# Value products of eight heads in one stretch, and a narrower price for products that run beside others, in a planned transformer block

## The chip, the cores and the metric

The kernel runs on one core of one Trainium2 chip. The core has TensorE (PE, matrix products; PEld are its weight loads), VectorE (DVE), ScalarE (ACT), GpSimd (POOL), and queues that issue DMAs, of which SyncE (SP) issues most here. The metric is the device time of one execution in microseconds, median of several runs. Before the change it is 1022.17 us (3 runs, 1020.41 to 1023.81).

## What is computed

One transformer block with 2048 tokens of width 640: layernorm, attention of 32 heads of width 20 over a sliding window of 256 tokens, a residual, a second layernorm and a gated feed-forward of width 1536.

```python
h  = x + A(layernorm(x))          # A: qkv = x @ wqkv; 32 heads, Dh = 20, W = 256
#   scores = q k^T * Dh**-0.5; masked to 0 <= i - j < 256; p = softmax(scores)
#   out = (p v) @ wo
h2 = h + B(layernorm(h))          # B: (gelu(x @ w_gate) * (x @ w_up)) @ w_down
```

## The kernel before

**Tiles.** Tokens are cut into 16 blocks of 128 (a chunk is two blocks). Dense products run in 16-bit pieces: each operand is split into a high and a low float16 part, and three products (high-high, high-low, low-high) stand for one. Of a block j, the window holds the key blocks j-2, j-1 and j.

**Attention, per block and pair of heads.** Four steps follow each other.

1. `maxima` writes q k^T of a pair of heads into one of two double banks of PSUM (`ra`, `rb`). Head dimensions are on 60 rows, so products run in quarters of the array: 2 row halves (the two heads) by 2 column halves. `max_out` then takes the row maximum on VectorE, one fused operation a head: add the mask (`band`, or `mask` for the first two blocks), reduce by max into a column of `mx`, and write the sum itself to a scratch tile `junk`, of which there is a single buffer. The profile shows it as CUSTOM_DVE_ANT_0, followed by a short read of the accumulator.
2. When a block has all 32 maxima, they are turned by a PE transpose (`max_transpose`) and put as two more rows under the queries, so that the next product comes out with the maximum subtracted. Maxima run some 20 pairs ahead of scores (`LEAD`).
3. `scores` computes k q^T of a pair into `ra` or `rb` (62 rows, 12 products for a full window). `score_out` takes the exponential on ScalarE into the probability tile `pt`. When all four heads of a unit `u` are there, GpSimd zeroes what the mask forbids, with three `affine_select` for a full window and one for the first two blocks. Then the unit is put into the queue `valq`. `pt` has 3 buffers of four heads.
4. `value_lane` multiplies a unit's probabilities with the values: for each key block four products side by side, one for each head, on 32 columns of the array each. A full window has 3 such groups; in float32 each product shows as two instructions, so a unit is x24 in the timeline (x16 and x8 for the first blocks). Results lie in the PSUM bank `pv`, four units in it; after each fourth unit ScalarE copies it to `oT`, and the unit after that waits for the copy.

In the timeline, products with shape 60*64 are maxima, 62*64 scores, 128*21 values, and 128*128 dense products or transposes. Maxima and scores together are called row products here, values column products, and a run of one kind a stretch.

**What sets the order.** The program is written out by a planner in the kernel itself. `Clock` keeps a time for each engine and a price for each instruction (`Engine.cost`, lines 214 to 250). Work sits in generators ("lanes"), each of which says what its next instruction needs; the loop at the end asks the lanes in an order of priority, and issues the first that can start by the planned clocks. The prices therefore only set the order of the instructions. For TensorE the price has three parts: `SWITCH` = 0.095 us where the kind of stretch changes, the columns at 2400 per us, and a fixed small price for a product that runs beside the one before it on another part of the array (`beside`). On VectorE the planner lets an operation that touches what the operation before it wrote start 0.1 us later (line 111).

Dense products (`dense_lane`) and attention are weighed by `ahead`: as long as the dense lane is ahead of the scores, attention comes first. Value products have two rules of their own. While the array is in row mode they come before nearly everything, and with fewer than two units waiting they are kept from starting out of dense products:

```python
if nc.mode == "row":
    early = [values] + early
elif len(valq) < 2 and (maxq or scoreq):
    att_lanes = [rows]
```

`row_need` starts row products by twos where both double banks come free within 1 us of each other; it lets scores start only while a probability buffer is free.

Before the scores begin, the loop also issues products with the identity (`pv<-ident` in the profile) whenever TensorE has nothing to do.

After attention, the first feed-forward group fills gaps (`first_feed_forward`), and then the rest of the feed-forward runs.

All instructions are recorded at line 199, where the helper issues them.

## Time and profile before

| | |
|---|---|
| median of 3 runs | 1022.17 us (1020.41 to 1023.81) |
| the profiled execution | 1023.17 us, of which its span is 1021.3 us |
| granted TensorE clock | 1.00 throughout |
| instructions | 30777 |
| probability masking (`affine_select` on `pt`) | 352 instructions, 175.3 us of GpSimd |
| maxima (CUSTOM_DVE_ANT_0) | 512 operations; 448 of them on 320 columns |
| value products | 2880 instructions, 104.1 us busy, from 92.2 to 574.1 us |
| DMA | 112.67 MB, mean 110 GB/s |

Busy times are shares of the span. A PE matmul's duration is longer than its pitch, since products are pipelined: a product of 320 columns lasts 0.30 us in the rows, and the next one starts 0.136 us after it. So the start times, not the durations, are added up for TensorE. A timeline row gives the start in us, the duration, the engine, the line, the operation with output and inputs, its shape and how many instructions were merged; a square bracket gives idle time before it and what ended that.

The stages can be told by the spans of the tiles: weights and the first layernorms up to about 50 us, maxima of the first blocks from 52 us, value products from 92 to 575 us, and feed-forward alone from there to the end.

### The profile page before, as it was taken

The page shows a single profiled execution, that of the slowest core. Times are in us where ns is not written, and L with a number is a line of the kernel's source. Part 1 is how long each engine was busy: PE and PEld are TensorE (multiplying, and loading weights), DVE is VectorE, ACT ScalarE, POOL GpSimd, SP SyncE. Part 2 cuts the span into 40 slices and gives each one's busy share as a digit, 9 for nine tenths or more (in the row PEclk, how much of TensorE's full clock was granted, in tenths as well). Part 3 has the DMA queues.
Part 4 walks back from the last instruction along what each step waited for, and adds up shares of the span by engine and source line. Part 5 has one row for each costly group of instructions (what it writes and reads, how often), then busy time and mean ns, then how long its engine had stood idle before and what let it go on. Part 6 is the DMA issues. An engine that isn't in the chain of part 4 may idle for free.

```text
span 1021.3 us, 30777 instructions
## 1 busy us (share of the span) xinstructions
PE 999.8 (98%) x12921; PEld 695.8 (68%) x12921; DVE 754.8 (74%) x2221; ACT 437.0 (43%) x706; POOL 298.0 (29%) x489
## 2 busy tenths in 40 slices
PE   8999999999999999999999999999999999999998
PEld 7875666676666676776655564567777777777776
DVE  6888998986787787474788788798996975544553
ACT  6514654656555564654558543522222222221220
POOL 7102223443343342342436321255313310000000
PEclk9999999999999999999999999999999999999999
DMA  8657667361551524225033433223553532222211
GB/s 306 137 116 175 184 145 168 81 163 55 91 122 44 114 57 118 42 61 127 3 131 106 92 117 103 78 104 127 161 177 90 161 138 78 78 96 86 78 53 52
DMA packets 105835, 112.67 MB, mean 110 GB/s; under 512 B 38369, under 2 KB 79585, under 8 KB 105697
## 3 DMA queue, kind: packets, MB, share of 16 engines
q1 hardware_dynamic: 93600, 99.97, 35.9%
q10 hardware_dynamic: 12096, 10.75, 3.4%
q8 instruction: 101, 1.65, 0.7%
q14 instruction: 38, 0.30, 0.1%
HBM read 73.73 MB, written 28.84 MB: 100 GB/s over the span
## 4 chain that ended last, share of the span: by engine, by line
PE 82%; DVE 8%; DMA 4%; ACT 2%; issue 2%; SPq 1%; POOL 0%; ACTq 0%; DVEq 0%
PE mm L199 41%; PE pv L199 12%; PE ra L199 11%; PE rb L199 10%; PE tp L199 7%; DVE junk L199 2%; DVE am L199 1%; DVE ht L199 1%; DMA v<-in_wqkv_dram 1%; DMA gu<-in_wqkv_dram 1%; SPq L199 1%; DMA qT<-mT 1%; DVE m L199 1%; ACT pt L199 1%; DMA h_dram<-ht 1%
## 5 line engine op out<-in xcount | busy, mean ns | idle before, releaser
L199 POOL TENSOR_SCALAR_AFFINE_SELECT pt<-pt 128x512 f32<-128x512 f32 x352 | 175.3, 513 | 278.2 <-ACT pt L199 262.6
L199 DVE CUSTOM_DVE_ANT_0 junk<-rb,band 128x320 bf16<-128x320 f32 x230 | 112.5, 489 | 41.3 <-PE rb L199 35.9
L199 DVE CUSTOM_DVE_ANT_0 junk<-ra,band 128x320 bf16<-128x320 f32 x218 | 106.6, 489 | 43.8 <-PE ra L199 38.3
L199 ACT ACTIVATE pt<-ra,esc 128x640 f32<-128x640 f32 (+2 forms) x131 | 99.6, 767 | 66.2 <-PE ra L199 53.3
L199 ACT ACTIVATE pt<-rb,esc 128x640 f32<-128x640 f32 (+2 forms) x125 | 94.9, 766 | 77.2 <-PE rb L199 56.5
L199 PE MATMUL pv<-pt,v 128*21 128x128 f32 x2880 | 104.1, 275 | 1.1 <-ACT oT L199 1.1
L199 PEld LDWEIGHTS <-ah 128*128 128x128 f16 x768 | 75.0, 98 | 29.5 <-issue 2.1
L199 ACT ACTIVATE gel<-gel,ffk 128x512 f32<-128x512 f32 x36 | 26.0, 721 | 138.0 <-DVE gel L199 138.0
L199 PEld LDWEIGHTS pv<-pt,v 128*21 128x21 f32 x2880 | 68.6, 100 | 11.9 <-issue 2.1
L199 PEld LDWEIGHTS <-ws 128*128 128x128 f16 x720 | 70.3, 98 | 8.3
L199 PEld LDWEIGHTS <-kT 62*64 62x64 f16 x2880 | 61.9, 107 | 13.9 <-issue 10.1
L199 PEld LDWEIGHTS <-qT 60*64 60x64 f16 x1280 | 29.8, 104 | 60.3 <-issue 51.3
L199 PEld LDWEIGHTS <-gu 128*128 128x128 f16 x440 | 42.1, 98 | 36.1 <-issue 2.5
L199 DVE SCALAR_TENSOR_TENSOR ht<-mm,ffk,ht 128x320 f32<-128x320 f32 x96 | 52.1, 545 | 10.9 <-PE mm L199 9.0
L199 ACT CAST ah<-gel 128x512 f16<-128x512 f32 x48 | 29.6, 617 | 64.4 <-DVE gel L199 64.2
L199 PE MATMUL mm<-xh,w1h 128*128 128x256 f16 x200 | 54.7, 274 | 1.3 <-DVE qks L199 1.3
L199 PE MATMUL mm<-xl,w1h 128*128 128x256 f16 x200 | 54.7, 273 | 0.0
L199 PE MATMUL mm<-xh,w1l 128*128 128x256 f16 x200 | 54.7, 273 | 0.0
L199 PE MATMUL mm<-w3l,oh 128*128 128x320 f16 x160 | 48.1, 301 | 0.1
L199 PE MATMUL mm<-w2h,xh 128*128 128x320 f16 x160 | 48.1, 300 | 0.0
L199 PE MATMUL mm<-w2h,xl 128*128 128x320 f16 x160 | 48.1, 301 | 0.0
L199 PE MATMUL mm<-w3h,ol 128*128 128x320 f16 x160 | 48.1, 300 | 0.0
(299 smaller groups left out, 2521.3 us busy)
## 6 DMA issues: line engine op xcount, KB each, us to landing
ws<-wsums SPq DMA_DIRECT2D x24, 640.0 KB
qk<-qks ACTq DMA_DIRECT2D x32, 256.0 KB
qT<-qk SPq DMA_DIRECT2D x48, 160.0 KB
kT<-qk SPq DMA_DIRECT2D x48, 160.0 KB
wsums<-ws SPq DMA_DIRECT2D x12, 640.0 KB
ht<-in_x_dram SPq DMA_DIRECT2D x16, 320.0 KB
h_dram<-ht SPq DMA_DIRECT2D x16, 320.0 KB
ht<-h_dram SPq DMA_DIRECT2D x16, 320.0 KB
```

Source lines behind the costliest of these rows:

```text
L199: r = real(*args, **kw)
```

## The change

Four things are changed, and the sizes that follow from them.

- **Values by eight heads.** `value_lane` waits for two units in `valq` and issues both, one after the other, in one step, with one check of `pv` for both.
- **Probabilities in halves.** `pt` becomes 7 buffers of two heads. Masking on GpSimd is done for each half as soon as its exponential is there, with the same number of instructions for two heads as before for four. Scores may start while a half is free.
- **No scratch tile.** The maximum operation writes its sum back to where it read it, in PSUM, in float32; `mask` and `band` are bfloat16; an unused tile `ones` goes.
- **The order's price** of a product beside another is 0.0005 us and not 0.004 us.

```diff
             if beside:
-                return 0.004
+                return 0.0005
...
-    ones = const.tile([P, P], F32, name="ones")
-    nc.vector.memset(ones, 1.0)
...
-    mask = wp.tile([P, 2 * P], F32, name="mask")
+    mask = wp.tile([P, 2 * P], BF16, name="mask")
...
-    band = wp.tile([P, 5 * HB], F32, name="band")
+    band = wp.tile([P, 5 * HB], BF16, name="band")
...
-    RV, RK = 5, 6
+    RV, RK, RP = 5, 6, 7
...
-        free = 3 - (pos["units"] - pos["values"])
+        free = RP - (pos["parts"] - 2 * pos["values"])
         for j, pr in list(scoreq)[:2]:
             b = B[j]
-            free -= pr % 2 == 0
+            free -= pairs(j)
...
-            junk = at("junk", [P, 5 * HB], BF16, 1)
-            nc.vector.tensor_tensor_reduce(junk[:, :w], head,
+            nc.vector.tensor_tensor_reduce(head, head,
                                            band if n == 3 else mask[:, (2 - n) * P:], 1.0,
...
-        u = pr // 2
-        if pr % 2 == 0:
-            b.pt[u] = at("pt", [P, 4, 3, P], F32, 3)
-            pos["units"] += 1
+        for k in range(pairs(j)):
+            b.pt[pr + k] = at("pt", [P, 2, 3, P], F32, RP)
+        pos["parts"] += pairs(j)
...
+        for k in range(pr, pr + pairs(j)):
+            pt = b.pt[k]
+            yield on("gpsimd", pt[:, :, 0, :])
+            if n == 3:
+                half = pt.rearrange("p h a (b c) -> p h (a b) c", b=2)
+                for a, (i, o) in enumerate(((0, 0), (3, 5))):
+                    nc.gpsimd.affine_select(half[:, :, o], half[:, :, i],
+                                            pattern=[[0, 2], [-1, HB]], compare_op=ALU.is_ge,
+                                            fill=0.0, base=-1 - HB * a, channel_multiplier=1)
+            diag = part(pt, n, n - 1).rearrange("p h a b -> p h (a b)")
+            nc.gpsimd.affine_select(diag, diag, pattern=[[0, 2], [1, P]],
+                                    compare_op=ALU.is_ge, fill=0.0, base=0, channel_multiplier=-1)
+            pos[j, "u", k // 2] += 1
+            if pos[j, "u", k // 2] == 2:
+                valq.append((j, k // 2))
...
-            yield pe(when=lambda: valq and B[valq[0][0]].v == 2 and pos["ones"])
-            j, u = valq.popleft()
+            yield pe(when=lambda: len(valq) > 1 and B[valq[0][0]].v == 2 and pos["ones"])
+            j, u = valq[1]
...
-            yield pe(pt, pv[:, u % 4, :])
-            for k, i in enumerate(order):
-                for c in range(4):
+            yield pe(*(b.pt[k] for k in range(2 * u - 2, 2 * u + 2)),
+                     pv[:, u % 4 - 1:u % 4 + 1, :])
+            for u in (u - 1, u):
+                valq.popleft()
+                pt = [b.pt.pop(k) for k in (2 * u, 2 * u + 1)]
+                for k, i in enumerate(order):
+                    for c in range(4):
...
-            pos["values"] += 1
+                pos["values"] += 1
```

The two rules of the loop for value products are left as they are.

More of the change, by code (lines that the diff above doesn't have):

```diff
@@ L977, in scores @@
         t = t[:, :, :pairs(j) * n * P]
-        tasks.append(score_out(j, pr, t, b.pt[u], at_))
+        tasks.append(score_out(j, pr, t, at_))
         pos["score"] += pairs(j)
@@ L986, in part, with score_out @@
         return (half[:, :, 0:6:5], half[:, :, 1:3], half[:, :, 3:5])[i]
-    def score_out(j, pr, t, pt, at_):
+    def score_out(j, pr, t, at_):
         b = B[j]
-        u = pr // 2
         n = len(window(j))
-        m = pairs(j)
+        w = min(n * P, 5 * HB)
         yield on("scalar", t)
-        w = min(n * P, 5 * HB)
-        for k in range(m):
-            h = 2 * (pr % 2 + k)
-            nc.scalar.activation(pt[:, h:h + 2].rearrange("p h a b -> p h (a b)")[:, :, :w],
+        for k in range(pairs(j)):
+            nc.scalar.activation(b.pt[pr + k].rearrange("p h a b -> p h (a b)")[:, :, :w],
@@ L998, in score_out @@
                                  t[:, :, k * n * P:k * n * P + w], AF.Exp, scale=esc)
         done(at_)
-        pos[j, u] += 2 * m
-        if pos[j, u] < 4:
-            return
-        yield on("gpsimd", pt[:, :, 0, :])
-        if n == 3:
-            half = pt.rearrange("p h a (b c) -> p h (a b) c", b=2)
-            for a, (i, o) in enumerate(((0, 0), (3, 5))):
-                nc.gpsimd.affine_select(half[:, :, o], half[:, :, i], pattern=[[0, 4], [-1, HB]],
-                                        compare_op=ALU.is_ge, fill=0.0, base=-1 - HB * a,
-                                        channel_multiplier=1)
@@ L1010, in score_out @@
-        diag = part(pt, n, n - 1).rearrange("p h a b -> p h (a b)")
-        nc.gpsimd.affine_select(diag, diag, pattern=[[0, 4], [1, P]],
-                                compare_op=ALU.is_ge, fill=0.0, base=0, channel_multiplier=-1)
-        valq.append((j, u))
+        for k in range(pr, pr + pairs(j)):
[13 more added lines that the diff above has]
+                valq.append((j, k // 2))
@@ L1024, in value_lane @@
             order = [1, 0, 2] if n == 3 else list(range(n))
[L1025 to L1032 removed]
+            yield pe(*(b.pt[k] for k in range(2 * u - 2, 2 * u + 2)),
[5 more added lines that the diff above has]
+                    for c in range(4):
+                        nc.tensor.matmul(pv[32 * c:32 * c + DH + 1, u % 4, :].rearrange(
+                                             "p (a b) -> p a b", b=HB),
+                                         vring[ks[i] % RV][:, 4 * u + c, :],
+                                         part(pt[c // 2], n, i)[:, c % 2],
+                                         start=(k == 0), stop=(k == n - 1))
+                pos["values"] += 1
             if u % 4 == 3:
```

7 lines of the change are left out of this document (1 added, 6 removed).

## The prediction

> **What bounds the kernel now.** I read the page first (busy times, chain, groups), then busy time by stretches of 50 us, then the timelines of TensorE and VectorE.
>
> ```profile
> PE 999.8 (98%) x12921; PEld 695.8 (68%) x12921; DVE 754.8 (74%) x2221; ACT 437.0 (43%) x706; POOL 298.0 (29%) x489
> ...
> PE 82%; DVE 8%; DMA 4%; ACT 2%; issue 2%; SPq 1%; POOL 0%; ACTq 0%; DVEq 0%
> ...
> L199 ACT ACTIVATE pt<-ra,esc 128x640 f32<-128x640 f32 (+2 forms) x131 | 99.6, 767 | 66.2 <-PE ra L199 53.3
> ...
> L199 PE MATMUL pv<-pt,v 128*21 128x128 f32 x2880 | 104.1, 275 | 1.1 <-ACT oT L199 1.1
> ```
>
> TensorE is busy 98% of the span, and 82% of the chain that ended last lies on it. The value products, which the change regroups, wait 1.1 us in all, and only for the copy to `oT`, never for GpSimd's masking. By stretches (PE, PEld, DVE, ACT, POOL busy):
>
> ```profile
> 50.00:100.00 50.00, 47.92 (x575) 32.82 (x572) 41.38 (x187) 15.23 (x34) 4.27 (x7) 1.00 0.63 144
> 100.00:150.00 50.00, 48.47 (x801) 33.26 (x794) 46.69 (x158) 29.71 (x52) 14.22 (x26) 1.00 0.64 155
> 500.00:550.00 50.00, 49.06 (x857) 29.37 (x857) 38.86 (x130) 32.43 (x49) 21.86 (x41) 1.00 0.25 84
> 900.00:950.00 50.00, 50.00 (x377) 36.53 (x376) 27.41 (x51) 10.83 (x17) 3.62 (x5) 1.00 0.29 104
> ```
>
> The second and third rows are the first and last of nine from 100 to 550, the attention: PE is busy 442.1 of 450 us there, DVE 344.4. From about 600 on PE has next to no gap. So the time is what TensorE has to do, plus some 8 us of gaps in attention; an edit counts if it takes work or switching from TensorE, or moves those gaps. An engine beside it matters only where it makes TensorE wait. Now TensorE's starts, for what one value stretch costs:
>
> ```profile
> 410.36 0.30 PE L199 MATMUL mm<-w2h,xh 128*128 128x320 f16 x1
> 410.49 0.30 PE L199 MATMUL mm<-w2l,xh 128*128 128x320 f16 x1
> 410.72 0.85 PE L199 MATMUL pv<-pt,v 128*21 128x128 f32 x24
> 411.50 0.34 PE L199 MATMUL ra<-qT,kT 62*64 62x128 f16 x12
> 411.67 0.31 PE L199 MATMUL rb<-qT,kT 62*64 62x128 f16 x12
> 411.91 0.85 PE L199 MATMUL pv<-pt,v 128*21 128x128 f32 x24
> 412.70 0.31 PE L199 MATMUL mm<-w2h,xl 128*128 128x320 f16 x1
> ```
>
> ```profile
> 102.21 0.42 PE L199 MATMUL pv<-pt,v 128*21 128x128 f32 x8
> 102.56 0.28 PE L199 MATMUL mm<-xh,w0l 128*128 128x256 f16 x1
> ```
>
> ```profile
> 424.44 0.33 PE L199 MATMUL ra<-kT,qT 60*64 60x256 f16 x8
> 424.61 0.31 PE L199 MATMUL rb<-qT,kT 62*64 62x128 f16 x12
> 424.85 0.28 PE L199 MATMUL mm<-xh,w0h 128*128 128x256 f16 x1
> ...
> 426.05 0.33 PE L199 MATMUL rb<-kT,qT 60*64 60x256 f16 x8
> ```
>
> A unit of three groups takes 0.79 us until the next dense product (411.91 to 412.70), one of a single group 0.35 us (102.21 to 102.56). So a group costs 0.22 us and the stretch as such 0.13 us. The score stretch before it takes 0.24 us whether values follow (411.67 to 411.91) or dense products (424.61 to 424.85): leaving row mode costs the same either way. Going into values out of dense products costs 0.09 us more: 410.49 to 410.72 is 0.23 us, the pitch of those products 0.14 us.
>
> **The change part by part.**
>
> *Values by eight heads.* There are 16 blocks of 8 units, 128 units, and in the timeline each now has a stretch of its own, nearly all right behind row products. Of two units the second takes three groups, 0.66 us, where it took 0.79 us: 0.13 us saved, times 64 pairs: 8.3 us. This holds if the pair starts behind row products. If it starts out of dense products the way in costs 0.09 us again and 0.04 us is left, 2.6 us in all. Which it is follows from the cadence. The last half's scores end at, say, 424.85; the exponential takes 0.77 us by its group, masking a half 1.00 us (below), which with 0.2 us for the handing over, my estimate, gives 426.8. The next row stretch starts at 426.05 and takes 0.41 us: it is over before the pair is ready. Where row stretches are 2 us apart, the pair comes just in time. And the loop's guard against starting out of dense products holds only for fewer than two units waiting, so it never holds for a pair. I take half and half: **-5.5 us**, ends -8.3 and -2.6.
>
> *Masking by halves* doubles the count.
>
> ```profile
> L199 POOL TENSOR_SCALAR_AFFINE_SELECT pt<-pt 128x256 f32<-128x256 f32 x224 | 89.9, 425 | 246.6 <-ACT pt L199 246.4
> L199 POOL TENSOR_SCALAR_AFFINE_SELECT pt<-pt 128x512 f32<-128x512 f32 x128 | 85.3, 667 | 31.7 <-ACT pt L199 16.3 <-issue 2.7 <-PE ra L199 2.5
> L199 POOL TENSOR_SCALAR_AFFINE_SELECT mask<-mask x1: 292/292/292, 1.8 to 1.8; 128x128 f32<-128x128 f32 x1
> ```
>
> 256 halves need one select of 256 elements each (0.42 us), and 224 of them two of 128 (0.29 us): 237 us where it was 175 us. GpSimd has the room, having stood idle 278 us before these very rows, and a unit is ready no later: its last half needs 1.00 us after its exponential, where the whole unit took 0.67 + 2 x 0.42 = 1.5 us. Cost 0 while that cover holds.
>
> *Seven halves instead of three units* is 14 heads in flight where 12 were, but freed eight at a time. While four halves wait for masking and values, three more scores may go; at 1.6 us a row stretch (424.44 to 426.05) that covers 4.8 us, against the 2 to 3.5 us that a pair waits. Cost 0; dense products fill the place of a held score.
>
> *No scratch tile.* On VectorE:
>
> ```profile
> 266.91 0.49 DVE L199 CUSTOM_DVE_ANT_0 junk<-rb,band 128x320 bf16<-128x320 f32 x1
> 267.32 0.08 DVE L199 DVE_READ_ACCUMULATOR2_ANT mxs<- 128x1 f32 x1
> 267.55 0.49 DVE L199 CUSTOM_DVE_ANT_0 junk<-ra,band 128x320 bf16<-128x320 f32 x1
> 267.97 0.08 DVE L199 DVE_READ_ACCUMULATOR2_ANT mxs<- 128x1 f32 x1
> 268.09 0.49 DVE L199 CUSTOM_DVE_ANT_0 junk<-ra,band 128x320 bf16<-128x320 f32 x1
> 268.50 0.08 DVE L199 DVE_READ_ACCUMULATOR2_ANT mxs<- 128x1 f32 x1
> 268.50 0.55 DVE L199 SCALAR_TENSOR_TENSOR ht<-mm,hsc,ht 128x320 f32<-128x320 f32 x1
> ```
>
> A maximum followed by another operation gives way after 0.41 us (268.09 to 268.50), one followed by a maximum after 0.54 us (267.55 to 268.09), across banks 0.64 us (266.91 to 267.55). All share `junk`, and the accumulator read comes at 0.41 us in every case, so I lay the 0.12 to 0.23 us to the wait for the scratch tile. Such neighbours number 211 in one bank and 20 across from 86 us on: 211 x 0.12 + 20 x 0.23 = 30 us of VectorE; in the ramp, 52 to 81 us, where its maxima follow each other without a gap, about 50 x 0.12 + 12 x 0.23 = 9 us. [...]
>
> The sum goes to PSUM now. Nearest row for such a write:
>
> ```profile
> 1.94 0.48 DVE L199 MEMSET pv<- 128x512 f32 x1
> ```
>
> [...] Reading and writing one bank in the same operation is in no row. Ends: nothing, or the write taking turns with the read, 0.48 x 320/512 = 0.30 us more for each of 448 maxima, 134 us. [...]
>
> What does a lighter VectorE bring? TensorE waits little for it. In the ramp it is filled with dummy products:
>
> ```profile
> 56.26 0.83 PE L199 MATMUL pv<-ident 128*128 128x128 f16 x12
> 56.93 0.27 PE L199 MATMUL mm<-xh,w0h 128*128 128x256 f16 x1
> ```
>
> ```profile
> L199 PE MATMUL pv<-ident x50: 218/220/231, 45.8 to 74.3; 128*128 128x128 f16 x50
> ```
>
> 50 at 0.056 us (12 of them take 0.67 us, 56.26 to 56.93) are 2.8 us; ends 0 and -2.8, I take **-1.4 us**. Of the 8 us of gaps in attention I take **-1 us**; ends -8, and +8 if the new order doubles them.
>
> *The order's price.* A stretch of 8 maxima and 12 scores has 15 products that run beside others; it was planned at 0.46 us and is now at 0.41 us, and the rows say 0.41 us (424.44 to 424.85). A value unit goes from 0.78 to 0.75 us against 0.79 us measured. On the whole the plan comes nearer. No instruction is added or removed; what it does to gaps is in the +-8 us. Halved mask tiles, and the lost `ones`, cost nothing in the stretch that counts.
>
> **Sum:** -5.5 - 1.4 - 1 = -7.9 us from the profiled execution's 1023.17 us (span 1021.3 us and 1.9 us around it): 1015.3 us. The median of the runs was 1.0 us below that execution, so **1014.3 us**.
>
> **The rivals.**
>
> 1. *Nothing to measure.* Pairs start mostly out of dense products (-2.6 us) and the new order's gaps eat the rest: 1019 to 1025 us. For it: the cadence above. Against: 0.04 us is still a gain.
> 2. *Slower: values wait for masking.* A pair needs its fourth half masked; the planner prices a half's three selects at 0.72 us where the rows give 1.00 us, and it starts the pair as soon as it thinks it ready. If TensorE stands 0.28 us before each of 64 pairs, that is 18 us: 1022.2 - 5.5 + 18 = 1035 us. It decides from 0.09 us a pair on (5.5/64). For it: pairs come free in the middle of dense products now, not at the next row stretch, so slack is gone. Against: before, the same price was short by 0.24 us (1.26 against 1.5 us) and no value product waited for GpSimd; and the planner adds 0.18 us at each hand-over.
> 3. *Slower: PSUM takes turns.* 134 us more on VectorE in attention: 344 + 134 = 478 us of work in 450 us, so attention ends some 30 us later, and the gaps that dense work does not fill, I guess half, cost 15 us: about 1030 us. [...]
> 4. *Faster still.* All pairs behind row products (-8.3), the dummies gone (-2.8), half the gaps gone (-4): 1007 us.
> 5. *It does not do what it says*: the wait between maxima stays, being the accumulator's. Then VectorE gains nothing and only the -5.5 us stand: 1016.7 us, inside the forecast.
>
> **How the numbers follow.** A measurement of this kernel can tell about 0.3%, 3 us, from no change. Forecast with rival 5, 1010 to 1019 us: 0.52. Rival 4, below 1010: 0.11. Rival 1: 0.18. Rival 2: 0.12, rival 3: 0.07. So faster 0.63, same 0.18, slower 0.19. The range from 1004 to 1028 us holds the first three cases and the milder part of 2 and 3, and leaves some 0.15 out. Likeliest case alone: 1010 to 1019 us.
>
> **What would show it.** Value stretches of x48, about 1.45 us to the next product, 64 of them, behind `62*64` rows in half of the cases. Maxima 0.41 to 0.42 us apart instead of 0.54; if 0.54 stays, the wait was the accumulator's; if single ones last 0.7 us or more, rival 3. GpSimd's masking near 237 us. If value products show idle time released by GpSimd, rival 2. The forecast is wrong if TensorE's gaps from 100 to 550 us grow beyond 13 us, or if stretches of TensorE outnumber those of before.

## The result and the profile after

The changed kernel takes 1027.77 us (median of 4 runs, 1027.3 to 1029.19) against 1022.08 us before on the same chip (1020.41 to 1023.81): ratio 1.0067, 95% interval 1.0051 to 1.0082. It is slower by some 6 us where 1014.3 us was forecast. 1027.8 us lies at the very end of the range. The granted clock is no part of the difference: its mean over an execution is 0.998 to 1.000 in the four runs, and 1.000 in the profiled execution before and after.

First the page of the changed kernel: busy times, the chain that ended last, and the groups that the prediction spoke of.

```profile
PE 998.1 (97%) x12910; PEld 701.4 (68%) x12910; DVE 767.3 (75%) x2220; ACT 434.2 (42%) x706; POOL 359.6 (35%) x841
...
PE 69%; DVE 17%; DMA 6%; issue 3%; ACT 2%; SPq 1%; POOL 1%; ACTq 0%; DVEq 0%; POOLq 0%
...
L199 POOL TENSOR_SCALAR_AFFINE_SELECT pt<-pt 128x128 f32<-128x128 f32 (+1 forms) x704 | 238.2, 356 | 238.0 <-ACT pt L199 215.0
L199 DVE CUSTOM_DVE_ANT_0 rb<-rb,band 128x320 f32<-128x320 f32 x222 | 110.5, 498 | 39.8 <-PE rb L199 22.9
...
L199 PE MATMUL pv<-pt,v 128*21 128x128 f32 x2880 | 92.2, 274 | 0.4 <-POOL pt L199 0.4
```

VectorE has become heavier (754.8 to 767.3 us) where it was to become some 39 us lighter, and its share of the chain went from 8% to 17%. GpSimd's masking costs 238 us, as worked out, and makes value products wait 0.4 us. Busy time by stretches (PE, PEld, DVE, ACT, POOL) shows where TensorE lost:

```profile
50.00:100.00 50.00, 43.23 (x546) 30.34 (x544) 43.37 (x181) 16.47 (x36) 8.48 (x18) 1.00 0.75 157
100.00:150.00 50.00, 48.12 (x714) 32.69 (x715) 48.51 (x167) 26.28 (x46) 13.27 (x33) 1.00 0.62 167
900.00:950.00 50.00, 50.00 (x375) 36.48 (x373) 24.45 (x46) 10.22 (x16) 4.35 (x6) 1.00 0.26 93
```

From 50 to 100 us PE is busy 43.23 us where it was busy 47.92 us; the late stretch is full, as before. So the loss is in the ramp and the attention. Added up from the start times, TensorE's time beyond the bare pitch of its products grew by some 6 us, about the span's 5 us. It can be divided only by an estimate of what a change of mode costs. From 88 to 580 us there are 93 changes fewer (625 to 532). One costs 0.09 us if taken from dense into row products (products of 320 columns start 0.14 us apart, the row product behind one of them after 0.23 us) and 0.13 us if taken from the prediction's value stretch: by these estimates switching between modes fell by 8 to 12 us, and waits grew by 14 to 18 us.

What VectorE does now, from the timeline:

```profile
261.93 0.50 DVE L199 CUSTOM_DVE_ANT_0 ra<-ra,band 128x320 f32<-128x320 f32 x1 [1.34 <-PE ra L199]
262.35 0.14 DVE L199 DVE_READ_ACCUMULATOR2_ANT mxs<- 128x1 f32 x1
262.52 0.50 DVE L199 CUSTOM_DVE_ANT_0 ra<-ra,band 128x320 f32<-128x320 f32 x1
262.94 0.14 DVE L199 DVE_READ_ACCUMULATOR2_ANT mxs<- 128x1 f32 x1
262.97 0.26 DVE L199 RECIPROCAL rec<-tp 128x16 f32<-128x16 f32 x1
```

Two maxima in one double bank stand 0.59 us apart (261.93 to 262.52) where it was 0.53 to 0.54 us; one followed by another operation still gives way after 0.42 to 0.45 us. Across banks the pitch fell from 0.64 to 0.42 us, but there are 14 such neighbours of 320 columns and 216 of the first kind. The wait was not taken away: it moved from the scratch tile to the double bank, a tile that a maximum now writes and that its neighbour reads, though in other columns (each head has its own 512). In both kernels the neighbour starts 0.03 to 0.04 us after the accumulator read between the two has ended (262.49 to 262.52 us here, 268.05 to 268.09 us in the prediction's rows). That read takes 0.14 us where it took 0.08 us, and this is the difference between 0.59 and 0.53 us.

One row shows what TensorE sees of that. The weight load with 60 rows comes first in a run of maxima's products; its last number groups are the idle time before it and what ended it. Before, then after, in the trace's groups by line:

```profile
L199 PEld LDWEIGHTS <-qT 60*64 60x64 f16 x1280 | 29.8, 104 | 60.3 <-issue 51.3 <-DVE mxs L199 4.5 <-DMA kT<-qk 1.0
```

```profile
L199 PEld LDWEIGHTS <-qT 60*64 60x64 f16 x1280 | 29.5, 104 | 66.8 <-DVE mxs L199 35.1 <-issue 28.4 <-DVE lvex L199 0.5
```

VectorE's maxima (`mxs`) now end 35.1 us of this idle time, where it was 4.5 us. Weight loads overlap products (in the page above PE is busy 97% of the span and PEld 68%), so this is no sum of lost time; it is a mark that tells how often TensorE comes to a double bank before VectorE is done with it, and it is used for that below. How much time is lost, it does not tell.

### The profile page after: what moved, and what is told of

Read it like the earlier page. It is cut to its first block, busy times and chain, and to the rows that moved or that the text cites. A ratio compares the mean times of both kernels' runs of the same rounds, so it can differ in the third digit from the quotient of the medians.

```text
span 1026.3 us, 31187 instructions
## 1 busy us (share of the span) xinstructions
PE 998.1 (97%) x12910; PEld 701.4 (68%) x12910; DVE 767.3 (75%) x2220; ACT 434.2 (42%) x706; POOL 359.6 (35%) x841
## 4 chain that ended last, share of the span: by engine, by line
PE 69%; DVE 17%; DMA 6%; issue 3%; ACT 2%; SPq 1%; POOL 1%; ACTq 0%; DVEq 0%; POOLq 0%
PE mm L199 32%; PE pv L199 11%; PE ra L199 11%; PE rb L199 9%; PE tp L199 6%; DVE ra L199 4%; DVE rb L199 4%; DVE mxs L199 2%; SPq L199 1%; DVE am L199 1%; DMA kT<-qk 1%; DMA qT<-mT 1%; DMA v<-in_wqkv_dram 1%; DMA wsl<-h_dram 1%; DVE ht L199 1%
## 5 line engine op out<-in xcount | busy, mean ns | idle before, releaser
L199 POOL TENSOR_SCALAR_AFFINE_SELECT pt<-pt 128x128 f32<-128x128 f32 (+1 forms) x704 | 238.2, 356 | 238.0 <-ACT pt L199 215.0
L199 DVE CUSTOM_DVE_ANT_0 rb<-rb,band 128x320 f32<-128x320 f32 x222 | 110.5, 498 | 39.8 <-PE rb L199 22.9
L199 DVE CUSTOM_DVE_ANT_0 ra<-ra,band 128x320 f32<-128x320 f32 x226 | 112.5, 498 | 31.2 <-PE ra L199 21.4
L199 ACT ACTIVATE pt<-rb,esc 128x640 f32<-128x640 f32 (+2 forms) x129 | 98.7, 772 | 79.2 <-PE rb L199 62.6
L199 ACT ACTIVATE pt<-ra,esc 128x640 f32<-128x640 f32 (+2 forms) x127 | 96.2, 764 | 69.6 <-PE ra L199 54.0
L199 PEld LDWEIGHTS <-ah 128*128 128x128 f16 x768 | 75.1, 98 | 28.5 <-issue 1.4
L199 PE MATMUL pv<-pt,v 128*21 128x128 f32 x2880 | 92.2, 274 | 0.4 <-POOL pt L199 0.4
L199 PEld LDWEIGHTS pv<-pt,v 128*21 128x21 f32 x2880 | 73.7, 101 | 13.1 <-issue 9.3
L199 PEld LDWEIGHTS <-qT 60*64 60x64 f16 x1280 | 29.5, 104 | 66.8 <-DVE mxs L199 35.1
L199 DVE DVE_READ_ACCUMULATOR2_ANT mxs<- 128x1 f32 x512 | 72.3, 141 | 0.0
L199 POOL TENSOR_TENSOR gelt<-gelt 128x256 f32<-128x256 f32 x18 | 15.2, 847 | 111.3 <-ACT gelt L199 111.3
L199 POOL TENSOR_TENSOR rr<-rr 128x256 f32<-128x256 f32 x18 | 14.2, 789 | 107.7 <-ACT rr L199 107.7
```

The costliest lines, as they stand in the source:

```text
L199: r = real(*args, **kw)
```

## The experiments

There are 18 runs of kernels. Each is compared with the kernel before on its own chip (medians 1022.08 to 1023.59 us), so ratios are what to compare; 0.1% is 1 us. The first four take the change apart: in them theory A says that the in-place write costs the time, B the order's price, C the pairs and halves.

**e1, the change with the scratch tile put back**

```diff
-            nc.vector.tensor_tensor_reduce(head, head,
+            junk = at("junk", [P, 5 * HB], BF16, 1)
+            nc.vector.tensor_tensor_reduce(junk[:, :w], head,
```

(`mT` has one buffer instead of two, to make room.)

> The changed kernel with one thing undone: the maxima write their sums to the bfloat16 scratch tile in SBUF again (one buffer; for room, the small tile mT has one buffer instead of two). Theory A (the write back into PSUM makes TensorE wait: a maximum that follows another in the same double bank starts 0.59 us after it where it was 0.53 us, while the planner believes 0.40 us): the switching saved stays, 54 us of it against 67 us, and the waits go back from 66 us towards 48 us: 1008 to 1014 us, and neighbours 0.53 us apart again. Theory B (the order's price of 0.0005 makes the waits) and theory C (values by eight heads and halves make them): 1025 to 1030 us.

1028.09 us, ratio 1.0048 (1.0025 to 1.0072), against 1.0067 for the change: the intervals overlap. The maxima stand as before (0.53, 0.64 us), and the kernel is no better for it that could be told. Theory A in its simple form falls.

**e2, the kernel before with the in-place write alone** (and bfloat16 masks)

```diff
-            junk = at("junk", [P, 5 * HB], BF16, 1)
-            nc.vector.tensor_tensor_reduce(junk[:, :w], head,
+            nc.vector.tensor_tensor_reduce(head, head,
```

> The kernel before with one thing done: the maxima write back into PSUM and the masks are bfloat16. Theory A: waits of TensorE rise by some 10 to 19 us, 1032 to 1041 us, neighbours in one double bank 0.58 to 0.59 us apart. Theories B and C: 1021 to 1024 us.

1054.31 us, ratio 1.0298 (1.0263 to 1.0333): 31 us slower, over five times the loss of the whole change, and beyond what any theory expected.

**e3, the kernel before with the order's price alone**

```diff
-                return 0.004
+                return 0.0005
```

> The kernel before with one thing done: the order's price of a product beside another is 0.0005 us. Theory A and theory C: the order changes a little, 1019 to 1024 us. Theory B: waits rise by 10 to 19 us, 1032 to 1041 us.

1024.18 us, ratio 1.0015 (0.9992 to 1.0038): nothing that can be told from no change, so theory B's number did not come.

**e4, pairs and halves alone** (with bfloat16 masks and without `ones`): the changed kernel with the scratch tile (one buffer of `mT`) and the price 0.004 us, so e1 with the other price.

```diff
-                return 0.0005
+                return 0.004
```

> The kernel before with values by eight heads and probabilities in halves alone: scratch tile kept (mT has one buffer for room), order's price 0.004 us, masks bfloat16. Theory A and theory B: switching falls from 67 to some 54 us and waits stay near 48 us, 1008 to 1014 us. Theory C: the waits rise with it, 1025 to 1030 us.

1012.42 us, ratio 0.9904 (0.9870 to 0.9937). So pairs and halves gain 10 us, as theories A and B expected. The parts do not add up: the price costs nothing on the kernel before and 1.4% on top of pairs; the in-place write costs 3% on the kernel before, and taking it out of the whole change gains nothing.

The parts share one thing: the planner. It prices a maximum of 320 columns at 0.065 + 0.00106 x 320 = 0.404 us, and a tile given anew starts 0.18 us after its last use (`Clock.tile` and `latest`). With the scratch tile neighbours are thus 0.58 us apart in the plan, 0.53 us on the chip; in place 0.40 us in the plan, which compares columns and finds nothing to wait for, and 0.59 us on the chip. For the next runs theory M says that this too low price makes the order bad; H, that the in-place write itself costs the time on the chip; C (the B of the first four) that it is the price of products beside others; S, that any edit sways the order.

**e5, the change with the price 0.004 us** (pairs and the in-place write)

```diff
-                return 0.0005
+                return 0.004
```

> The change with its price for products beside others put back from 0.0005 to 0.004 us: pairs and halves with the in-place maximum. Pairs alone gave 1012.4 us, the in-place write alone 1054.3 us, the whole change 1027.8 us. Theory M (the planner prices a run of maxima at 0.40 us apiece once the scratch tile is gone, where the chip takes 0.59 us, and so brings row products to TensorE before VectorE can have freed their banks): the loss of 31 us is there whatever the values do: 1035 to 1045 us. Theory C (the loss of the whole change is the price, as it is 15.7 us from pairs alone to pairs with the price): 1010 to 1015 us. Theory S (the order is made greedily, and any edit moves the gaps by about 10 us one way or the other): no number, anywhere from 1010 to 1045 us.

1041.35 us, ratio 1.0170 (1.0133 to 1.0207). Theory M's number came out: the in-place write with its planned order costs 2.7% on top of pairs, as it cost 3.0% without them. And within the change the lower price gains 1%.

**e6, the change with dearer maxima in the plan**

```diff
         if self.name == "vector":
             m = max([n] + [i.free_size() for i in ins])
+            if op == "tensor_tensor_reduce":
+                return 0.065 + 0.00106 * m + 0.1
```

> The whole change, but the planner reckons 0.1 us more for each maximum, 0.50 us for 320 columns, which is about the mean of 0.59 us next to one in the same bank and 0.42 us else. The instructions are those of the change in another order. Theory M: the waits that came with the change, 18.6 us on TensorE, mostly go: 1008 to 1016 us. Theory H (the in-place maximum holds its bank for 0.59 us and this is what costs time, whatever the order): no gain, 1024 to 1031 us. Theory C (price for products beside others): 1024 to 1031 us as well.

1032.93 us, ratio 1.0078 (1.0052 to 1.0103). Theory M missed: no gain, and the time is above every theory's range. The mark by the weight loads fell (`mxs` 35.1 to 9.9 us), but another gap opened, which e9 explains.

**e7, the in-place write alone with dearer maxima in the plan**: e2 with e6's edit.

```diff
+            if op == "tensor_tensor_reduce":
+                return 0.065 + 0.00106 * m + 0.1
```

> The kernel before with the in-place maximum (1054.3 us), with 0.1 us more for each maximum in the plan. The plan then reckons what it reckoned of the kernel before, 0.50 us a maximum. Theory M: 1018 to 1027 us, next to the kernel before. Theory H: 1045 to 1055 us, since the maxima are the same ones. Theory S: anything between.

1031.37 us, ratio 1.0077 (1.0052 to 1.0102): 2.2 of the 3.0% are gone with the maxima unchanged in kind, by the planned price alone. The time lies between the ranges of M (up to 1027 us) and H (from 1045 us). The expectation's claim that the plan then reckons what it reckoned of the kernel before was wrong: that is 0.58 us between neighbours, and here it was 0.50 us.

**e8, the kernel before with cheaper maxima in the plan**

```diff
+            if op == "tensor_tensor_reduce":
+                return 0.065 + 0.00106 * m - 0.1
```

> The kernel before with its scratch tile and nothing of the change, but the planner reckons each maximum 0.1 us cheaper, so that a run of maxima is planned at 0.40 us apiece as it is in the kernel with the in-place write; the chip goes on taking 0.53 us. Theory M: slower by about two thirds of 31 us, 1040 to 1048 us, with TensorE standing for VectorE. Theory H: 1020 to 1027 us, since no instruction has changed. Theory S: anything between.

1050.06 us, ratio 1.0250 (1.0221 to 1.0278). No part of the change is in this kernel, its maxima take what they took, and it is 26 us slower, 2 us more than M's range. (Between neighbours the plan has 0.48 us, not the 0.40 us of the expectation.) Theory H can't make this; M can. The mark for e4, e2 and e8, in this order, from the groups by line:

```profile
L199 PEld LDWEIGHTS <-qT 60*64 60x64 f16 x1280 | 30.5, 104 | 61.7 <-issue 55.9 <-DVE mxs L199 2.2 <-DMA kT<-qk 0.9
```

```profile
L199 PEld LDWEIGHTS <-qT 60*64 60x64 f16 x1280 | 29.4, 104 | 69.1 <-DVE mxs L199 44.8 <-issue 18.9 <-DVE am L199 0.7
```

```profile
L199 PEld LDWEIGHTS <-qT 60*64 60x64 f16 x1280 | 29.9, 104 | 58.7 <-DVE mxs L199 33.1 <-issue 21.3 <-DVE ht L199 0.5
```

A plan that thinks VectorE faster than it is sends TensorE to row products whose bank is not free yet. Since e6 fits M badly, the next runs take in theory T: that the order can be wrong on either side, with row products too soon or with the dense products used up too soon.

**e9, pairs alone with maxima a little dearer in the plan**

```diff
+            if op == "tensor_tensor_reduce":
+                return 0.065 + 0.00106 * m + 0.03
```

> Pairs alone with the scratch tile (1012.4 us), the planner reckoning 0.03 us more for each maximum: 0.53 us from one maximum to the next, which is what the chip takes. The instructions are those of pairs alone. Theory T (two faults of the order, one on either side: with maxima priced too low TensorE stands for VectorE; with row products held back longer, dense products run ahead of the attention and are used up near 460 us, after which TensorE has too little to put between the row stretches, as in pairs with the price, where it was busy 7.1 and 6.0 of 10 us at 460 and 490 us): a price nearer the truth makes it slower, 1023 to 1030 us, with TensorE idle some 15 us between 450 and 500 us. Theory M alone (only too low a price does harm): 1010 to 1015 us.

1026.50 us, ratio 1.0034 (1.0010 to 1.0057). Theory T's number came out, and M alone falls: too dear does harm as well, of another kind. (Planned neighbours are 0.61 us apart here, not 0.53 us: the price went away from the truth, not nearer.) In ten us each at 460 and 490 us, pairs alone (e4) and then this run:

```profile
460.00:470.00 10.00, 10.00 (x211) 6.81 (x208) 6.42 (x25) 5.95 (x12) 5.52 (x18) 1.00 0.79 138
490.00:500.00 10.00, 10.00 (x209) 7.13 (x211) 6.24 (x26) 5.67 (x9) 5.24 (x17) 1.00 0.39 150
```

```profile
460.00:470.00 10.00, 7.13 (x166) 5.29 (x156) 5.71 (x23) 4.55 (x6) 5.04 (x16) 0.66 0.59 139
490.00:500.00 10.00, 6.76 (x142) 4.89 (x138) 6.15 (x25) 5.12 (x7) 4.74 (x16) 0.83 0.84 292
```

PE is busy 7.13 and 6.76 of 10 us, with no engine full, and its granted clock (the number behind POOL's) is 0.66 and 0.83 there. From 450 to 500 us PE stands idle for 7 us by busy time, where T had 15 us, and the mean granted clock is 0.90 where it is 1.00 in e4, by an estimate from these two numbers (0.10 of 50 us) another 5 us. The dense products (tile `mm`; PE busy) from 450 to 500 us, in e4, e1 and e9:

```profile
450.00:500.00 50.00, 28.93 (x172) 0.00 (x0) 1.63 (x3) 3.48 (x8) 1.00 0.45 121
```

```profile
450.00:500.00 50.00, 17.97 (x108) 0.00 (x0) 2.19 (x4) 1.74 (x4) 0.95 0.44 110
```

```profile
450.00:500.00 50.00, 16.01 (x89) 0.00 (x0) 2.19 (x4) 0.87 (x2) 0.90 0.47 121
```

There are 11 to 13 us fewer of them. In the timeline of e1 row stretches then follow each other with nothing between:

```profile
492.88 0.31 PE L199 MATMUL rb<-qT,kT 62*64 62x128 f16 x12
494.50 0.33 PE L199 MATMUL rb<-kT,qT 60*64 60x320 f16 x4 [1.31 <-ACT pt L199]
494.63 0.34 PE L199 MATMUL ra<-qT,kT 62*64 62x128 f16 x12
495.93 0.33 PE L199 MATMUL ra<-kT,qT 60*64 60x320 f16 x4 [0.96 <-ACT pt L199]
496.06 0.34 PE L199 MATMUL rb<-qT,kT 62*64 62x128 f16 x12
```

TensorE then waits for the exponential, because it has no dense work to cover it. This is what e6's gap was too: 7.11 and 7.13 us of 10 at the same places. In the code the projections end about there, and the feed-forward's weights are loaded only once all projections are issued (`dense_lane` opens their pool); that this is why the dense work runs out was read from the code and not tried.

**e10, pairs and in place, price 0.004 us, dearer maxima in the plan**

```diff
-                return 0.0005
+                return 0.004
...
+            if op == "tensor_tensor_reduce":
+                return 0.065 + 0.00106 * m + 0.1
```

> The change with the price for products beside others at 0.004 us (1041.4 us so far) and 0.1 us more for each maximum in the plan. Theory T: maxima are priced about right and the dense products do not run out, since the price is the old one: 1010 to 1020 us. Theory M: the same, 1010 to 1018 us. Theory H (the in-place maxima themselves cost TensorE time): 1025 us or more, as the whole change with the true price took 1032.9 us. Theory S (sway without a pattern): 1010 to 1045 us.

1021.33 us, ratio 0.9993 (0.9967 to 1.0019): 1.8%, some 18 us, better than e5 by the plan's price, 9 us worse than pairs alone. It lies between the numbers of T or M and that of H.

**e11, in place and price, no pairs**: e2 with the price 0.0005 us.

```diff
-                return 0.004
+                return 0.0005
```

> The kernel before with the in-place maximum and the price of 0.0005 us, no pairs: the change without its values by eight heads. In place alone gave 1054.3 us, the price alone 1024.2 us. Theory T (the lower price makes TensorE's stretches shorter in the plan, so it waits longer for VectorE there and puts more dense products between row stretches, which takes back part of what too cheap maxima cost; with pairs it took back 13.6 of 29 us): 1036 to 1046 us. Without such an offset: 1053 to 1057 us.

1047.64 us, ratio 1.0233 (1.0182 to 1.0283). The price takes back 0.65% of 3%; the sign was right, the size below what T expected. The one price does +1.4% (e4 to e1), +0.15% (e3), -0.65% here and -1.0% (e5 to the change): its worth depends on which side the order is wrong.

**e12, e10 with the price raised to 0.008 us**

```diff
-                return 0.004
+                return 0.008
```

> The change with the price for products beside others raised to 0.008 us and 0.1 us more for each maximum. Theory T: further from the side on which dense products run out, with the maxima priced about right: 1008 to 1018 us, as with 0.004 us or some us better. If the price of products beside others does harm in either direction from 0.004 us: 1020 us or more.

1026.41 us, ratio 1.0043 (1.0010 to 1.0075). Theory T missed; the number of the other expectation, that the price does harm on either side of 0.004 us, came out. Neither of T's marks is there: dense work is at hand at 460 and 490 us, and `mxs` ends 5.6 us of the weight loads' idle time. Three single waits stand out in the timeline: 5.2 and 2.5 us for the copy of keys (`kT`) and 3.3 us for an exponential. The last of them costs more than its length: behind it the granted clock was 0.50 for 3 us with PE full. Around it:

```profile
153.00:156.40 3.40, 0.17 (x2) 0.10 (x1) 1.23 (x4) 1.40 (x3) 0.00 (x0) 0.99 1.06 239
156.50:159.50 3.00, 3.00 (x28) 2.17 (x28) 2.38 (x7) 1.82 (x3) 2.03 (x5) 0.50 0.71 177
```

Such waits come and go with the order (4.8 us once in e3, 2.8 us once in e4), and no price in these runs accounts for them: so much of theory S holds.

**e13, the kernel before with two scratch tiles**, and the unused tile gone

```diff
-            junk = at("junk", [P, 5 * HB], BF16, 1)
+            junk = at("junk", [P, 5 * HB], BF16, 2)
```

> The kernel before with two scratch tiles in turn instead of one (room made by halved mask tiles and without the unused tile of ones). The planner sees no wait between neighbouring maxima and reckons 0.40 us apiece, as with the in-place write (1054.3 us); here a maximum waits at most for the one before the last. If the wait is the scratch tile's alone, maxima stand 0.42 us apart in every place. Theory M: the plan's price is then near the truth and the 31 us are not there: 1018 to 1026 us; as far below 1022.5 as a lighter VectorE is worth anything, for which the prediction had 2.4 us. If the wait is the accumulator's (the prediction's fifth rival), maxima stay 0.53 us apart, the price is too low and the time is that of the kernel before planned too cheap, 1045 to 1055 us. Theory S: anything between.

1024.21 us, ratio 1.0021 (1.0006 to 1.0036). Page and timeline:

```profile
PE 999.3 (98%) x12907; PEld 699.3 (68%) x12907; DVE 726.3 (71%) x2220; ACT 436.4 (43%) x706; POOL 297.2 (29%) x489
```

```profile
263.23 0.49 DVE L199 CUSTOM_DVE_ANT_0 junk<-ra,band 128x320 bf16<-128x320 f32 x1 [0.53 <-PE ra L199]
263.65 0.08 DVE L199 DVE_READ_ACCUMULATOR2_ANT mxs<- 128x1 f32 x1
263.65 0.49 DVE L199 CUSTOM_DVE_ANT_0 junk<-ra,band 128x320 bf16<-128x320 f32 x1
264.06 0.08 DVE L199 DVE_READ_ACCUMULATOR2_ANT mxs<- 128x1 f32 x1
```

This is what the change meant to do: no wait, maxima 0.41 to 0.42 us apart everywhere, VectorE 28.5 us lighter (754.8 to 726.3 us), and the plan's 0.40 us true. It brings nothing: the time is 0.6 to 3.7 us above that of the kernel before. A part of that may be the clock, whose mean over an execution is 0.990 to 0.998 here (median 0.995) and 0.998 to 1.000 in the runs of the kernel before on this chip (median 1.000); by an estimate, 0.005 of 1022 us is up to 5 us.

The run shows more when it is set beside e2. In both the planner sees no wait between maxima. The traces have every operation of VectorE, ScalarE and GpSimd in the same order (one memset fewer here), and TensorE's weight loads too, but for three more loads of the identity for dummy products, and two of these and one transpose moved by some places, all before the first scores. So one and the same order takes 1.0298 when a maximum makes its neighbour wait in the double bank, and 1.0021 when it does not: the order of e2 is no bad one, it is bad for maxima that take 0.59 us instead of the 0.40 us planned. The mark alone would not have told this, as it stays high in e13:

```profile
L199 PEld LDWEIGHTS <-qT 60*64 60x64 f16 x1280 | 29.1, 104 | 53.4 <-DVE mxs L199 22.8 <-issue 22.5 <-DVE rec L199 1.8
```

**e14 and e15, the scratch tile in one stage and in place in the other**

```diff
+            junk = head if W["v"].ready else at("junk", [P, 5 * HB], BF16, 1)[:, :w]
+            nc.vector.tensor_tensor_reduce(junk, head,
```

(e15 with the two choices changed over; planned 0.1 us dearer where in place; price 0.004 us.)

> Pairs and halves with the price 0.004 us; the maxima write to the scratch tile until the weights of the values are split, near 85 us, and in place after that, each planned near what the chip takes (0.50 us). All in place took 1021.3 us, all with the scratch tile 1012.4 us. If the in-place write costs its 9 us in the ramp, where VectorE goes from maximum to maximum: 1011 to 1016 us. If in the attention behind it: 1018 to 1023 us.

1022.17 us, ratio 1.0001 (0.9984 to 1.0017).

> The mirror image: maxima in place until the weights of the values are split, then with the scratch tile. If the in-place write costs its 9 us in the ramp: 1017 to 1023 us. If in the attention: 1010 to 1015 us. Both of these runs near 1016 us would share it out; both near 1012 or both near 1021 us would make it sway of the order.

1013.11 us, ratio 0.9916 (0.9898 to 0.9935). These runs do not tell what they were made for: the condition held from the first maximum, so in the trace all 512 maxima of e14 are in place and all of e15 use the scratch tile. They are e10 and e4 once more on another chip, and repeat them to about 0.1%.

**e16, e17, e18: the order held fixed.** The planner sees one output and the chip writes another, so every engine has the instructions of the parent in the same order (the traces bear this out), and only the place of the maxima's output differs. Theory O says that the order made without the scratch tile is what costs.

```diff
-            r = real(*args, **kw)
+            r = real(*([kw.pop("to"), *args[1:]] if "to" in kw else args), **kw)
...
-                                           b.mx[:, par * 16 + pr + k:par * 16 + pr + k + 1])
+                                           b.mx[:, par * 16 + pr + k:par * 16 + pr + k + 1], to=head)
```

(The planner is given `junk`. e16 is this on e4, e17 on the kernel before. e18 is the reverse on the whole change: the planner is given `head`, the chip `junk`.)

> The order of pairs alone (scratch tile in the plan, 1012.4 us), instruction by instruction, with the maxima written in place. Theory O (the loss lies in the order that the planner makes once the scratch tile is gone): within 3 us of pairs alone, 1010 to 1016 us. Theory H (the write to PSUM costs the 9 us that stayed when the plan's price was raised to 0.50 us): 1019 to 1024 us.

1014.44 us, ratio 0.9914 (0.9886 to 0.9942), against 0.9904 and 0.9916 for its parent.

> The order of the kernel before, instruction by instruction, with the maxima written in place. The in-place write with an order of its own took 1054.3 us, and 1031.4 us with 0.50 us planned for a maximum. Theory O: 1020 to 1026 us, the time of the kernel before. Theory H: 1029 to 1034 us.

1023.91 us, ratio 1.0014 (0.9992 to 1.0035).

> The order of the whole change (1027.8 us), instruction by instruction, with the maxima written to a scratch tile on the chip, which the plan does not see. Theory O: the order keeps its loss; neighbouring maxima in one double bank take 0.53 us instead of 0.59 us, across banks 0.64 us instead of 0.42 us, so 0.06 x 216 - 0.22 x 14 = 10 us of VectorE less, of which TensorE sees the part that it waits for: 1022 to 1028 us. Theory H: the write to PSUM was the loss: 1012 to 1019 us.

1021.41 us, ratio 0.9985 (0.9963 to 1.0008), against 1.0067 for the change.

Two orders made for the scratch tile bear the write to PSUM at next to no cost, though in both its neighbours stand 0.59 us apart and the accumulator read is the longer one; so theory H's 9 us are not in the write as such, and both runs meet theory O. In e16 the mark stays low in spite of the heavier VectorE (766.7 us busy):

```profile
L199 PEld LDWEIGHTS <-qT 60*64 60x64 f16 x1280 | 30.6, 104 | 62.5 <-issue 54.8 <-DVE mxs L199 4.0 <-DMA wsl<-in_wu_dram 0.6
```

In the change's own order the write costs 0.8% (e18 against the change, each against its own chip); the mark is high with and without it (27.1 us in e18). e18 comes out just below O's range (1022 to 1028 us) and above H's (1012 to 1019 us): in an order that brings row products early, the 0.06 us more between neighbours is felt. And that order costs 0.7 to 0.8% even with the scratch tile (0.9985 against 0.9904 of e4 and 0.9916 of e15). So the write costs next to nothing in e16 and e17, 0.8% here, and 2.8% in the order that e2 and e13 share.

## Why the prediction was wrong, step by step

Put together, in ratios to the kernel before: pairs and halves 0.9904; with the change's order, but the scratch tile on the chip, 0.9985; with the write to PSUM, 1.0067. That is -1.0%, +0.8% and +0.8%. That the time still lies inside the stated range is partly luck. The 8 us that the prediction allowed for the gaps of a new order, and rival 1 with them, are of the right kind, but order and write together cost twice that, and it was the larger gain of the pairs that brought the time back into the range.

- **Values by eight heads: right, and too small.** -5.5 us was forecast with -8.3 us as the best end; e4 gains 9.8 us (0.96% of 1022.95 us; interval 6 to 13 us). The stretch is as worked out. In the timeline of the change:

```profile
190.14 0.30 PE L199 MATMUL mm<-w3l,oh 128*128 128x320 f16 x1
190.37 1.51 PE L199 MATMUL pv<-pt,v 128*21 128x128 f32 x48
191.81 0.33 PE L199 MATMUL rb<-kT,qT 60*64 60x320 f16 x4
```

  1.44 us for 48 products, 1.45 us forecast; of the 64 stretches 56 are of this kind, 4 have 32 products and 4 have 16. What was missed is probably the way out: in e4 24 of the 64 stretches start right behind row products and in the change 15, where half were expected, but 39 and 40 run on into row products, as here, and save the return to dense mode. By the prediction's prices the starts alone would be worth 24 x 0.13 + 40 x 0.04 = 4.7 us in e4. Counted in the traces from 88 to 580 us, changes of mode fell from 625 to 541 in e4 and to 532 in the change. The prediction priced only how a pair begins. That the rest of the 9.8 us is the way out is read from these counts; no run tries it, and none parts the pairs from the halves.
- **Masking by halves and seven halves: right.** 238.2 us against 237 us forecast, and a 0.4 us wait of value products for GpSimd; rival 2 did not occur.
- **"No scratch tile": the step that failed.** The prediction put it so: "All share `junk`, and the accumulator read comes at 0.41 us in every case, so I lay the 0.12 to 0.23 us to the wait for the scratch tile." That cause was right (0.53 us with one tile, in the kernel before, and 0.41 us once two take turns, in e13). But it took for granted that without the tile nothing is left to wait for. A maximum that writes into its double bank makes its neighbour there wait, 0.59 us, and 216 of 230 neighbours of 320 columns are of that kind. Why the program makes it wait, though the two heads have different columns, no run tries. So VectorE became 12.5 us heavier instead of some 39 us lighter. The test that the prediction gave, that a remaining wait would be the accumulator's (rival 5), would have misled: e13 has the same accumulator reads and no wait. Where there is a wait, it ends with that read, and so the longer read made it longer. The sum has no term for a longer maximum, and that was right: one lasts 498 ns where it lasted 489 ns, so rival 3, the write taking turns with the read, was wrong.
- **The gains from a lighter VectorE (-1.4 and -1 us) did not come.** e13 has the light VectorE and is no faster. From 45.5 us on it has 38 of the dummy products where the kernel before has 54; at the prediction's 0.056 us each that is 0.9 us. What a faster VectorE buys in the ramp shows in the first score product. Before, in the change and in e13 it starts at:

```profile
90.03 0.31 PE L199 MATMUL ra<-qT,kT 62*64 62x128 f16 x8
```

```profile
79.18 0.31 PE L199 MATMUL rb<-qT,kT 62*64 62x128 f16 x8
```

```profile
73.51 0.31 PE L199 MATMUL rb<-qT,kT 62*64 62x128 f16 x8
```

  Attention begins 11 and 16.5 us earlier, and TensorE is busy less from 50 to 100 us: 43.23 us in the change and 45.00 us in e13, against 47.92 us. The early start leaves TensorE with gaps that were not there before, and in e13 the clock falls as well: it was 0.50 from 80 to 85 us, after five us in which TensorE was busy 2.72 us, and products of 256 columns started 0.21 us apart there (82.89 to 85.03 us) and 0.11 us apart from 86.97 us on. In the change it stayed at 1.00. What a lighter VectorE would bring without these gaps, no run shows.
- **"The order's price": costed at 0, "on the whole the plan comes nearer".** The second step that failed: the prediction weighed what a price says against the rows, one at a time. What matters is the balance of two prices, against what the chip takes. The planner puts dense products between row stretches until VectorE is due; with maxima planned cheaper than they are, TensorE is sent to row products too soon and waits for `mxs` (e2, e5, e8 and the change), and where the chip keeps the planned price, the same order loses 0.2% and not 3.0% (e13 beside e2); with maxima dear, or TensorE's own products cheap, dense products are used up and are missing near 460 us (e1, e6, e9). The change tipped both prices at once, and neither loss is what either edit costs by itself. The prediction looked at the scratch tile as VectorE's time alone and did not see that the planner reads its price from it.
- **What would show it.** The signs named for a wrong forecast did not come, and were badly chosen. TensorE's gaps from 100 to 550 us were to grow beyond 13 us: by busy time they grew from 7.9 to 9.9 us, since a product's duration overlaps the next one (1.51 us for the 48 value products above, 1.44 us to the next start) and hides short waits; by the estimate from start times the waits there grew by 9 to 10 us, and from 50 to 100 us, which the sign left out, by 4 to 7 us. Stretches of TensorE were to outnumber those of before: they became fewer. What did tell was the pitch of the maxima, and it took a value that no sign had named, 0.59 us.

What stays open: the single waits of 2 to 5 us for key copies in some orders; how the gain of e4 divides between pairs and halves; how the 0.8% of the change's order divides between its two prices; and whether a better balance exists. The fastest kernel of the study is e4, pairs and halves without the in-place write and the new price, 1.0% below the kernel before and 1.6% below the changed one.

## What to carry to other kernels

When a buffer is taken away to get rid of a wait, look for what the new output is shared with: here a write in place tied the next reader of that tile to it. Where a planner sets the order, a dependency that goes is also a price that goes; hold the order fixed and change only the operation on the chip, then change only the price, before either is believed. And VectorE, which ended 8% of the chain, brought nothing when it was made 28.5 us lighter (e13): ask first what the engine that is full would do with the time.

## What the runs showed of the hardware

- The accumulator read behind a maximum takes 82 to 83 ns when the maximum writes to SBUF and 141 ns when it writes to PSUM (e13 and the change, groups by line). The type changes with the place, from bfloat16 to float32, and no run parts the two.

```profile
L199 DVE DVE_READ_ACCUMULATOR2_ANT mxs<- 128x1 f32 x512 | 42.1, 82 | 0.0
```

```profile
L199 DVE DVE_READ_ACCUMULATOR2_ANT mxs<- 128x1 f32 x512 | 72.3, 141 | 0.0
```

- The maximum itself, 320 elements in PSUM in and out in float32, takes 498 ns against 485 to 489 ns with a bfloat16 output to SBUF: here reading and writing one bank at once was nearly free. What costs is the wait of the neighbour, which starts 0.03 us after the accumulator read's end, 0.17 us beyond the 0.42 us after which another operation starts.
- Where TensorE was short of work the granted clock of the same ten us was below 1.00: at 460 and 490 us 0.66 and 0.83 in e9, with PE busy 7.13 and 6.76 of 10 us, 0.83 and 0.67 in e6 (7.11 and 7.13 us), 0.86 and 0.90 in e1 (7.09 and 6.03 us); in e4, with PE busy 10.00 us, it was 1.00. Behind single waits it was 0.50 for some us: behind 3.3 us in e12 (rows above), behind 2.84 us in e13 (0.50 from 80 to 85 us) and behind 2.2 us in e10 (0.50 from 294.8 to 298 us). Behind the longest wait of the change between 45 and 600 us, 2.0 us at 86 us, it stayed at 1.00.
